# A first attention chunk that skips the operand split, and a written-out order for every engine, in a fused attention and MLP kernel

## The chip, the core and the metric

The kernel runs on one core of one Trainium2 chip. The metric is the device time of one execution in microseconds (us), as a median of several runs. The core has five instruction streams that matter here: TensorE (PE, matmuls and transposes), VectorE (DVE), ScalarE (ACT), GpSimd (POOL) and SyncE (SP), which issues the DMAs. Each works through its own instructions in the order in which they were emitted and waits for semaphores of the others.

## What is computed

Attention over 4 batches, 8 heads, 768 positions and head size 64, with a mask and a bias, followed by a two-layer MLP with a GELU. The mask keeps the first `n_global` keys and the last `n_local` ones before each query.

```python
rel = pos[:, None] - pos[None, :]
is_global = pos[None, :] < int(n_global)
is_local = (rel >= 0) & (rel < int(n_local))
dist = np.where(is_global & ~is_local, float(n_local), np.abs(rel))
scores = scale * q @ k.T - slopes[:, None, None] * dist
a = softmax(np.where(is_global | is_local, scores, -1e9))
x = (a @ v).transpose(0, 2, 1, 3).reshape(3072, 512)
out = gelu(x @ w_in) @ w_out          # 512 -> 2048 -> 512
```

All operands are float32 on the host except the MLP weights, which come as 64-bit words.

## The kernel before

The 3072 tokens are cut into 12 chunks of 256; a batch is three of them. The program has two parts. In the first part all chunks go through attention and through the first two of the eight 256-wide slices of the hidden layer; at the same time the 64-bit weights are turned into float32 and split, and the other six slices are stored to DRAM. In the second part the six slices are multiplied with larger token blocks (lines 575 and 633).

All work is a list of named steps, each registered by `op` with the engines that may do it, an estimated duration, the steps it depends on and the buffers that it takes and frees. `schedule` places them in time on a model of the five engines and so fixes the engine, the order and the buffer of each; `emit` writes the instructions out in that order, and each engine is held to it. The letters, with a chunk, then a head or a pair of heads:

- `l` loads a pair of heads of a chunk (K, Q and V in one tile `nat`), `S` computes scores on TensorE (line 248), `R` adds the mask and takes the maximum on VectorE (265), `E` is the exponential on ScalarE (278), `U` the inverse of the sums (284, 286), `N` scales the rows (294 on ScalarE, 296 elsewhere), `T` transposes them on TensorE (305), `C` copies the result out of PSUM (213), `A` multiplies it with V (326).
- `X` and `Y` (`x_high`, `x_low`) split the attention output into a rounded high part `xh` and a rest `xl`; `W` adds the two again on GpSimd (346) and `Z` spills the sum to DRAM for the second part.
- `w` loads weight words, `D`, `F`, `j` and `J` turn 64-bit words into float32 (`J` is `round_word`, the last), `H` and `L` split them, `Q`, `h`, `o` and `B` prepare and store the other slices.
- `m` is the first layer on chunk and slice: three matmuls for each product (high times high, high times low, low times high); for chunk 0 in parts, one for each pair of heads (`m1_part`, line 472), for the others line 460. `G` and `K` are the GELU and its split, `n` the second layer (496), `O` and `ps` copy and store the partial result. `p` and `m2` are products of the second part.
- `lim` (`reach_of_limits`, lines 60 and 197 to 202) builds the mask out of `n_local` and `n_global`, which lie in the last words of the first `nat` tile; `P` (`penalties`, 252) scales the mask for each head.

Before the first scores TensorE runs idle matmuls (line 271, `warm`): ten, and more wherever the plan has a gap of over 0.5 us before the planned time `IDLE`, 19.761 us. The PSUM bank that they write is free for other use from then on.

Heuristics decide the order: a due time for each step, corrections by kind and chunk (`NUDGE`, `BIAS`), and, for TensorE from the third chunk on, a repeated pattern of seats (`SEATS`, `STEADY`).

Of the kernel before, what the change touches and what calls it, by code (L numbers as in the profile page):

```python
# [17 lines left out]
P = 128  # L18
# [23 lines left out]
W0, W1 = 772, 1280  # L42
# [22 lines left out]
def slope(h):  # L65
# [5 lines left out]
SLOTS = {"k": 8, "nat": 6, "pn": 10, "pt": 10, "x": 3, "xw": 1, "ws": 4, "wa": 4, "wst": 2, "sums": 1, "g": 3, "o": 2,  # L71
# [6 lines left out]
BIAS_FRONT = {("POOL", "N"): -0.807, ("POOL", "J"): -0.4, ("POOL", "L"): -0.546, ("POOL", "Q"): -0.235, ("POOL", "o"): -0.065, ("POOL", "D"): -0.221,  # L78
# [3 lines left out]
STEADY = (10.086, 44.882)  # L82
SEATS = {"S": [-2.0, -1.84, 0.0, 0.16],
         "T": [0.4, 0.48, 0.56, 0.64, 1.85, 2.56, 2.64, 2.93],
         "A": [1.6, 1.76, 3.6, 3.76],
         "m": [4.45, 4.53, 4.61, 4.69],
         "n": [7.2, 7.28, 7.44, 8.44]}
# [7 lines left out]
ISSUE, RATE, FETCH, LAND, AHEAD, CHK = .42, 350.0, 1.3, 1.3, 5.0, 2  # L95
FREE = (3.4, 2.5, 3.0, 2.0, .8)
NUDGE = {("R", 2): -2.16, ("R", 3): 4.48, ("E", 0): -3.31, ("E", 1): -4.66, ("E", 3): 1.13, ("U", 2): 0.06,
# [4 lines left out]
DEC = {(s, i): 57.774 + 6.435 * (4 * (s - NA) + i) for s in range(NA, NST) for i in range(4)}  # L102
EARLY_KEYS = {("A", 1): -0.91, ("A", 3): -0.65, ("m", 1): -0.46, ("m", 2): -0.43, ("n", 0): -0.23, ("n", 2): -1.11}
KEYS = {
    "S": lambda g: g + -1.156 + EARLY_KEYS.get(("S", g // 4), 0.0),
    "T": lambda g: g + 0.62 + EARLY_KEYS.get(("T", g // 4), 0.0),
# [28 lines left out]
class Fast:  # L135
# [197 lines left out]

    def x_high(self, e, c, p, n):
        av, xh, _ = self.x_views(c, p, n)
        self.copy(e, xh, av)
# [12 lines left out]
    def spill(self, c):  # L349
        self.nc.sync.dma_start(self.xd[c], self.t["xw", c].rearrange("p d t -> p (d t)"))  # L350
# [113 lines left out]
    def m1_part(self, c, s, d):  # L464
        xh, xl = self.t["xh", c], self.t["xl", c]
        wh, wl = self.win[s]
        if d == 0:
            self.bank(("h", c, s), [P, 2, CT])
        hp = self.t["k", ("h", c, s)]
        for f in range(2):  # L470
# [224 lines left out]
    def first_part(self):  # L695
        op = self.op
        for h in range(H):
            op(("P", h), [("DVE", .37), ("POOL", .54)], lambda e, h=h: self.penalties(e, h), [("lim",)], port=True)
        op(("lim",), ("DVE", 1.6), lambda e: self.reach_of_limits(), [("l", 0, 0)], free=[("nat", (0, 0))], port=True)
# [6 lines left out]
        for c in range(NCH):  # L706
            f = c % CPB == 0
            for p in range(NP):
# [3 lines left out]
                   kb=(384, 640)[not f])  # L712
                op(("S", c, p), ("PE", (.86, .66)[f]), lambda e, c=c, p=p: self.scores(c, p), [("l", c, p)],
# [9 lines left out]
                for h in (2 * p, 2 * p + 1):  # L723
# [8 lines left out]
                   [("C", c, 2 * p), ("C", c, 2 * p + 1), ("l", c, p), self.at("A", c, p - 1)],  # L732
# [739 lines left out]
```

## Time and profile before

| | us |
|---|---|
| median of 3 runs | 656.88 |
| lowest and highest | 656.49, 657.86 |
| the profiled execution | 656.78 |
| its span, first to last instruction | 655.0 |

| engine | busy us | share of the span |
|---|---|---|
| TensorE | 640.1 | 98% |
| VectorE | 531.0 | 81% |
| ScalarE | 445.5 | 68% |
| GpSimd | 186.8 | 29% |

The shares are averages over both parts. Matmuls are pipelined, and their busy time overlaps; the distance from one start to the next tells what one costs. Lines of a timeline merge neighbours of the same kind: the first number is the start, the second the time until the last of them ends.

### The profile page before, as it was taken

The numbers are of one execution on the slowest core, as the hardware profiler recorded it, in microseconds if no ns is written. First come the engines' busy times: TensorE is split into PE (matmuls) and PEld (weight loads), VectorE is DVE, ScalarE is ACT, GpSimd is POOL, SyncE is SP. The second block draws the span as 40 slices with busy tenths as digits, with TensorE's granted clock in tenths as the row PEclk, the third lists the DMA queues.
The fourth block names the chain that finished last, engine by engine and source line by source line (L and its number), as shares of the span: only waits on it lengthen the run. The fifth ranks groups of instructions, "written<-read, shape, count | busy, mean of one in ns | idle before, by whom it ended". The sixth has DMA issues, their size and how long they took to land. (4 is left out here: it accounts for less than half of the span.)

```text
span 655.0 us, 14882 instructions
## 1 busy us (share of the span) xinstructions
PE 640.1 (98%) x5359; PEld 597.1 (91%) x5359; DVE 531.0 (81%) x1546; ACT 445.5 (68%) x1141; POOL 186.8 (29%) x239
## 2 busy tenths in 40 slices
PE   9999999999999999999999999999999999999996
PEld 7788887888887888989999999999999999999996
DVE  8989999999979874555598789688977987896775
ACT  6999999999999999535554464456345544654450
POOL 5667758788876573100000000000000000000002
PEclk9999999999999999999999999999999999999999
DMA  8875698989979879979995979688888979786402
GB/s 305 290 236 199 258 338 343 344 316 357 394 282 329 324 246 380 419 274 397 419 405 208 327 275 365 240 308 325 312 297 298 333 268 322 263 313 202 172 1 69
DMA packets 48752, 192.44 MB, mean 294 GB/s; under 512 B 5408, under 2 KB 5920, under 8 KB 41760
## 3 DMA queue, kind: packets, MB, share of 16 engines
q1 hardware_dynamic: 48384, 191.16, 79.5%
q8 instruction: 44, 0.72, 0.4%
q14 instruction: 36, 0.29, 0.1%
q10 hardware_dynamic: 288, 0.26, 0.1%
HBM read 150.50 MB, written 40.89 MB: 292 GB/s over the span
## 5 line engine op out<-in xcount | busy, mean ns | idle before, releaser
L633 PE MATMUL k<-w,go 128*128 128x256 f32 x1512 | 193.7, 282 | 1.6 <-DVE vw L642 0.7
L633 PEld LDWEIGHTS k<-w,go 128*128 128x128 f32 x1512 | 185.0, 189 | 2.7 <-PE k L575 1.3
L575 PE MATMUL k<-xch,w1a 128*128 128x256 f32 x576 | 110.5, 284 | 0.5 <-DVE hc L585 0.5
L642 POOL TENSOR_TENSOR part<-part,r 128x256 f32<-128x256 f32 x1 | 0.7, 740 | 372.1 <-DVE r L642 372.1
L278 ACT ACTIVATE pn<-pn,nmax 128x256 f32<-128x256 f32 (+1 forms) x192 | 92.0, 483 | 5.8 <-DVE nmax L265 5.7
L575 PEld LDWEIGHTS k<-xch,w1a 128*128 128x128 f32 x576 | 92.5, 191 | 1.1 <-DVE hc L585 0.7
L575 PE MATMUL k<-xch,w1b 128*128 128x256 f32 x432 | 91.4, 282 | 0.5 <-ACT hc L581 0.5
L581 ACT COPY hc<-k 128x256 f32<-128x256 f32 x108 | 39.8, 368 | 67.9 <-PE k L575 67.8
L575 PE MATMUL k<-xcl,w1a 128*128 128x256 f32 x288 | 81.4, 283 | 0.0
L617 ACT CAST go<-gb 128x384 fp32r<-128x384 f32 x72 | 36.9, 513 | 54.6 <-PE k L633 54.1
L575 PEld LDWEIGHTS k<-xch,w1b 128*128 128x128 f32 x432 | 73.1, 191 | 0.7 <-ACT hc L581 0.7
L585 DVE TENSOR_TENSOR hc<-hc,k 128x256 f32<-128x256 f32 x108 | 44.8, 416 | 35.5 <-ACT hc L581 26.1
L593 ACT ACTIVATE gb<-hc 128x256 f32<-128x256 f32 x108 | 45.2, 418 | 40.6 <-DVE hc L585 39.6
L296 POOL TENSOR_SCALAR pn<-pn,ninv 128x256 f32<-128x256 f32 (+1 forms) x114 | 61.9, 558 | 32.5 <-DVE ninv L286 19.3
L265 DVE CUSTOM_DVE_ANT_0 pn<-k,pens 128x256 f32<-128x256 f32 (+1 forms) x192 | 66.0, 395 | 5.1 <-PE k L248 4.6
L575 PE MATMUL k<-xcl,w1b 128*128 128x256 f32 x216 | 60.9, 282 | 0.0
L305 PE MATMUL k<-ident,pn 128*128 128x128 f32 x352 | 52.7, 279 | 2.7 <-DVE pt L213 1.2
L216 DVE TENSOR_TENSOR go<-gb,go 128x384 fp32r<-128x384 f32 x72 | 39.8, 553 | 19.2 <-ACT go L617 18.8
L575 PEld LDWEIGHTS k<-xcl,w1a 128*128 128x128 f32 x288 | 55.1, 191 | 0.0
L460 PE MATMUL k<-xh,winh 128*128 128x256 f32 x176 | 52.3, 297 | 0.3 <-DVE nmax L265 0.3
L376 POOL TENSOR_TENSOR wa<-wa,ws 128x512 int32<-128x512 int32 x32 | 44.1, 1383 | 25.5 <-DVE wa L371 9.9
L305 PEld LDWEIGHTS k<-ident,pn 128*128 128x128 f32 x352 | 38.3, 140 | 14.0 <-issue 4.6
(123 smaller groups left out, 1458.2 us busy)
## 6 DMA issues: line engine op xcount, KB each, us to landing
w1a<-w1d SPq DMA_DIRECT2D x36, 1024.0 KB, 7.2
w1b<-w1d SPq DMA_DIRECT2D x36, 768.0 KB, 4.7
nat<-qkv SPq DMA_DIRECT2D x32, 640.0 KB, 6.4
ws<-w SPq DMA_DIRECT2D x32, 512.0 KB, 5.6
c<-w SPq DMA_DIRECT2D x64, 256.0 KB, 5.0
w1d<-wst SPq DMA_DIRECT2D x6, 1792.0 KB, 7.6
w2d<-wst SPq DMA_DIRECT2D x6, 1792.0 KB, 8.0
nat<-qkv SPq DMA_DIRECT2D x16, 386.0 KB, 4.6
```

Source lines behind the costliest of these rows:

```text
L216: self.eng(e).tensor_tensor(out=out, in0=in_, in1=hi.bitcast(F32), op=ALU.subtract)
L265: self.nc.vector.tensor_tensor_reduce(out=nn[:, j, :w], in0=sp[:, j, :w], in1=pen, scale=-0.125, scalar=3e38, op0=ALU.add, op1=ALU.min, ac ...
L278: self.nc.scalar.activation(out=nn[:, j, :w], in_=nn[:, j, :w], func=AF.Exp, bias=self.nmax[:, k, i:i + 1], scale=-1.0, accum_out=self.nsu ...
L296: self.eng(e).tensor_scalar(out=nn[:, j, :w], in0=nn[:, j, :w], scalar1=by, scalar2=0.0, op0=ALU.mult, op1=ALU.add)
L305: self.nc.tensor.transpose(tp[:, i, :], nn[:, j, a * P:(a + 1) * P], self.ident)
L376: self.eng(e).tensor_tensor(out=a, in0=a, in1=self.t["ws", (s, i)][:, :, 0], op=ALU.add)
L460: nc.tensor.matmul(hp[:, f, :], lhsT=w[:, d, f * P:(f + 1) * P], rhs=x[:, d, :], start=n == 0, stop=n == 3 * NP - 1)
L575: self.nc.tensor.matmul(out, lhsT=w[:, i, d * P:(d + 1) * P], rhs=y[:, d, :], start=bool(new) and n == 0, stop=n == 5, skip_group_check=no ...
L581: self.nc.scalar.copy(x, self.t["k", ("x", u)])
L585: self.nc.vector.tensor_tensor(out=x, in0=x, in1=self.t["k", (bank, u)], op=ALU.add)
L593: self.nc.scalar.activation(out=out, in_=src, func=AF.Gelu)
L633: self.nc.tensor.matmul(out[k], lhsT=o[:, i, a], rhs=w[:, b, j], start=s == 0 and n == 0 and k in (1, 4, 5, 6), stop=s == NB - 1 and n == ...
```

## The change

Four things change.

1. **The first chunk's loads.** The tiles of chunk 0 (and of the first chunk of each batch, in DRAM) have the limits behind K and Q instead of at the end. For chunk 0, `l` loads 516 words a row (K, Q and the limits) and a new step `v` loads the 256 words of V, which only `A` needs.
2. **The mask.** `reach_of_limits` has one VectorE operation less, and `penalties` may run on ScalarE too.
3. **Chunk 0 whole.** For chunk 0 the attention output is copied as it is (`x_copy`), with no `Y` and no `W`, and `Z` spills that copy. `m1_part` multiplies it with the unsplit float32 weight words in one matmul where three stood. It waits for `X` and `J` instead of `Y` and `L`. The weight words have 7 buffers instead of 4.
4. **The order.** `PLAN` lists, for each of the five engines, the steps of the first part and of the start of the second in their order (358 on TensorE, 370 on ScalarE, 527 on VectorE, 152 on GpSimd, 173 DMAs or pool openings on SyncE). A step in the table goes to the engine in whose list it stands, in that order, and the limits on PSUM use aren't asked for. Estimates of durations and latencies change; `IDLE` goes from 19.761 to 9.87. What is behind the table is ordered by `schedule` as before.

```diff
-SOON, SLACK, WINDOW, LAT, LAT0, IDLE = 0.0, 0.1, 12, 0.255, .05, 19.761
+SOON, SLACK, WINDOW, LAT, LAT0, IDLE = 0.0, 0.1, 12, 0.2, .1, 9.87
+WHOLE = 1
+PLAN = {
+    "PE": """
+        S:0.0 S:0.1 S:0.2 S:1.0 S:0.3 T:0.1 T:0.0 S:1.1 A:0.0 T:0.3 T:0.4 T:0.2 A:0.1 T:0.5 T:1.0 T:1.1 A:0.2 S:1.2
+        T:0.6 T:0.7 m:0.0.0 T:1.3 S:1.3 A:1.0 S:2.0 m:0.1.0 m:0.0.1 T:1.2 m:0.0.2 A:1.1 A:0.3 T:1.5 T:1.7 m:0.0.3
+        m:0.1.1 T:1.4 m:0.1.2 T:1.6 S:2.2 A:1.2 S:2.1 A:1.3 S:2.3 T:2.0 T:2.1 m:0.1.3 n:0.0.1 S:3.0 A:2.0 T:2.2 m:1.0.0
...
+    "ACT": """
+        P:1 P:7 E:0.0 E:0.1 E:0.2 E:0.3 E:0.4 E:0.5 C:0.1 E:1.0 E:1.1 E:0.6 C:0.3 E:0.7 E:1.2 D:0.0 E:1.3 X:0.1 N:0.6
+        C:1.1 D:0.1 N:1.3 C:1.0 C:0.6 C:0.7 D:1.0 E:1.5 E:1.4 D:1.1 E:1.6 E:1.7 C:1.2 H:0.0 E:2.1 D:0.2 X:0.3 D:0.3
...
+    "DVE": """
+        lim: P:0 R:0.0 R:0.1 R:0.2 R:0.4 R:0.3 U:0.0 R:0.5 R:1.0 R:1.1 U:0.1 R:0.6 R:0.7 U:0.2 C:0.0 R:1.3 R:1.2 U:1.0
+        N:1.1 F:0.0 C:0.2 X:0.0 U:0.3 F:0.1 C:0.4 C:0.5 j:0.0 F:1.0 J:0.0 U:1.1 j:0.1 F:1.1 j:1.0 R:1.5 R:1.4 X:0.2
...
+    "POOL": """
+        P:2 P:4 P:3 P:5 P:6 N:0.1 N:0.0 N:0.2 N:0.3 N:0.4 N:0.5 N:1.0 N:0.7 J:0.1 N:1.2 J:1.0 N:1.5 J:1.1 N:1.6 N:1.4
...
+    "SP": """
+        l:0.0 l:0.1 l:0.2 l:1.0 v:0.1 v:0.0 l:0.3 l:1.1 v:0.2 w:0.0 v:0.3 w:0.1 w:1.0 l:1.2 w:1.1 l:1.3 l:2.0 w:0.2
...
     def reach_of_limits(self):
...
-        nc.vector.tensor_scalar(out=col, in0=col, scalar1=self.ng, scalar2=BIG, op0=ALU.is_lt, op1=ALU.mult)
-        nc.vector.tensor_scalar(out=col, in0=col, scalar1=-BIG, scalar2=self.nl, op0=ALU.add, op1=ALU.subtract)
-        nc.vector.tensor_tensor(out=pen[:, 2 * P:], in0=pen[:, P:2 * P], in1=col, op=ALU.max)
-        nc.vector.tensor_copy(pen[:, 0:NG], col[:, 0:NG])
+        nc.vector.tensor_scalar(out=col, in0=col, scalar1=self.ng, scalar2=-BIG, op0=ALU.is_ge, op1=ALU.mult)
+        nc.vector.scalar_tensor_tensor(out=pen[:, 2 * P:], in0=col, scalar=self.nl, in1=pen[:, P:2 * P],
+                                       op0=ALU.subtract, op1=ALU.max)
+        nc.vector.tensor_scalar(out=pen[:, 0:NG], in0=col[:, 0:NG], scalar1=self.nl, scalar2=None, op0=ALU.subtract)
...
+        if c == 0:
+            self.nc.sync.dma_start(t[:, 0:WQ], self.qkv0[b, p, :, 0:WQ])
+            return
...
+    def load_values(self, p):
+        self.nc.sync.dma_start(self.t["nat", (0, p)][:, WQ:W0], self.qkv0[0, p, :, WQ:W0])
...
+        if e == "ACT":
+            self.nc.scalar.activation(out=self.pens[:, h], in_=self.pen, func=AF.Copy, scale=8.0 * slope(h))
+            return
...
+    def x_copy(self, e, c, p):
+        av, xh, _ = self.x_views(c, p, 1)
+        self.copy(e, xh.bitcast(F32), av)
...
     def spill(self, c):
-        self.nc.sync.dma_start(self.xd[c], self.t["xw", c].rearrange("p d t -> p (d t)"))
+        x = self.t["xh", c].bitcast(F32) if c < WHOLE else self.t["xw", c]
+        self.nc.sync.dma_start(self.xd[c], x.rearrange("p d t -> p (d t)"))
...
     def m1_part(self, c, s, d):
...
+        if c < WHOLE:
+            w = self.t["wa", (s, d // 2)].bitcast(F32)
+            for f in range(2):
+                self.nc.tensor.matmul(hp[:, f, :], lhsT=w[:, d % 2 * 256 + f * P:d % 2 * 256 + (f + 1) * P],
+                                      rhs=self.t["xh", c].bitcast(F32)[:, d, :], start=d == f == 0, stop=d == NP - 1,
+                                      skip_group_check=True)
+            return
```

## Rows read from the trace of the kernel before

**Rows 1.** Busy time by stage: engine (instructions) in us, then granted clock, DMA share, GB/s.
```profile
5.00:44.00 39.00, 36.86 (x336) 29.67 (x336) 35.83 (x153) 35.88 (x111) 26.45 (x43) 1.00 0.83 294
44.00:140.00 96.00, 93.75 (x790) 79.15 (x789) 88.83 (x256) 92.58 (x245) 70.67 (x79) 1.00 0.80 287
140.00:260.00 120.00, 118.58 (x1006) 102.17 (x1005) 100.67 (x316) 118.16 (x322) 82.12 (x104) 1.00 0.90 335
...
290.00:649.00 359.00, 356.38 (x2977) 354.56 (x2976) 286.27 (x783) 183.44 (x438) 3.81 (x5) 1.00 0.77 280
```

**Rows 2.** Timeline of VectorE, 4 to 7 us: start, us, engine, line, operation.
```profile
4.08 0.16 DVE L60 SCALAR_TENSOR_TENSOR nn<-nat 128x2 f32<-128x2 int32 x1 [1.15 <-DMA nat<-qkv]
...
4.87 0.28 DVE L199 TENSOR_SCALAR ta<-ta,nn 128x128 f32<-128x128 f32 x1
5.19 0.28 DVE L200 TENSOR_SCALAR ta<-ta,nn 128x128 f32<-128x128 f32 x1
...
5.92 0.74 DVE L252 TENSOR_SCALAR pens<-pen 128x384 bf16<-128x384 bf16 x2
6.78 0.29 DVE L265 CUSTOM_DVE_ANT_0 pn<-k,pens 128x128 f32<-128x128 f32 x1
```

**Rows 3.** Timeline of ScalarE: the first exponentials, and the last of chunk 1.
```profile
7.12 0.40 ACT L278 ACTIVATE pn<-pn,nmax 128x128 f32<-128x128 f32 x1 [5.11 <-DVE nmax L265]
...
8.01 0.39 ACT L278 ACTIVATE pn<-pn,nmax 128x128 f32<-128x128 f32 x1
...
30.98 0.50 ACT L278 ACTIVATE pn<-pn,nmax 128x256 f32<-128x256 f32 x1
...
32.95 0.50 ACT L278 ACTIVATE pn<-pn,nmax 128x256 f32<-128x256 f32 x1
```

**Rows 4.** Timeline of TensorE up to 22 us.
```profile
1.18 4.00 PE L271 MATMUL idle<-wz 128*128 128x256 f32 x17 [1.18 <-DVE wz L1239]
5.10 3.87 PE L248 MATMUL k<-nat 64*128 64x128 f32 x32
...
15.63 0.88 PE L326 MATMUL k<-pt,nat 128*64 128x128 f32 x12 [0.36 <-DVE pt L213]
...
21.93 0.63 PE L305 MATMUL k<-ident,pn 128*128 128x128 f32 x4 [0.88 <-DVE pt L213]
```

**Rows 5.** Timeline of TensorE, later steps.
```profile
25.17 1.75 PE L326 MATMUL k<-pt,nat 128*64 128x128 f32 x28
26.85 0.66 PE L305 MATMUL k<-ident,pn 128*128 128x128 f32 x4
27.26 0.36 PE L472 MATMUL k<-xh,winh 128*128 128x256 f32 x1
...
28.06 0.60 PE L305 MATMUL k<-ident,pn 128*128 128x128 f32 x4
28.59 2.01 PE L248 MATMUL k<-nat 64*128 64x256 f32 x16
...
43.76 0.39 PE L460 MATMUL k<-xh,winh 128*128 128x256 f32 x1
...
283.24 0.39 PE L496 MATMUL k<-wouth,gh 128*128 128x512 f32 x1
...
284.61 0.39 PE L496 MATMUL k<-wouth,gh 128*128 128x512 f32 x1
```

**Rows 6.** Groups by line, 0 to 290 us: count, busy us, mean ns, idle before.
```profile
L213 ACT COPY pt<-k 128x512 f32<-128x512 f32 (+1 forms) x55 | 29.4, 563 | 4.3 <-PE k L305 3.9
L371 DVE SCALAR_TENSOR_TENSOR wa<-ws,wa 128x512 int32<-128x512 int32 x32 | 25.1, 783 | 0.2
L213 DVE COPY pt<-k 128x512 f32<-128x512 f32 (+1 forms) x41 | 24.9, 616 | 1.3 <-PE k L305 1.1
L296 POOL TENSOR_SCALAR pn<-pn,ninv 128x256 f32<-128x256 f32 (+1 forms) x114 | 61.9, 558 | 32.5 <-DVE ninv L286 19.3
...
```

**Rows 7.** One microsecond of the front: engines' busy time, clock, DMA share, GB/s.
```profile
3.00:4.00 1.00, 1.00 (x7) 1.00 (x6) 0.00 (x0) 0.00 (x0) 0.00 (x0) 1.00 1.06 423
```

More of the change, by code (lines that the diff above doesn't have):

```diff
@@ L94 @@
 TABLE = 1.283
[L95 to L97 removed]
[4 rows of a table removed]
[L102 to L103 removed]
+ISSUE, RATE, FETCH, LAND, AHEAD, CHK = .42, 360.0, .8, 1.8, 5.0, 2
@@ L697, in first_part @@
         for h in range(H):
-            op(("P", h), [("DVE", .37), ("POOL", .54)], lambda e, h=h: self.penalties(e, h), [("lim",)], port=True)
-        op(("lim",), ("DVE", 1.6), lambda e: self.reach_of_limits(), [("l", 0, 0)], free=[("nat", (0, 0))], port=True)
+            op(("P", h), [("DVE", .25), ("POOL", .54), ("ACT", .45)], lambda e, h=h: self.penalties(e, h), [("lim",)], port=True)
+        op(("lim",), ("DVE", 1.5), lambda e: self.reach_of_limits(), [("l", 0, 0)], free=[("nat", (0, 0))], port=True)
         lag = KEYS
@@ L749, in first_part @@
                        alloc=[("xw", c)] if p == 1 else [], free=[("x", c)], due=(("A", c, p), 12.0))
-            op(("Z", c), ("SP", ISSUE), lambda e, c=c: self.spill(c), [("W", c, 0), ("W", c, 1)], free=[("xw", c)], kb=512, due=(("A", c, 3), 16.0))
+            op(("Z", c), ("SP", ISSUE), lambda e, c=c: self.spill(c),
+               [("X", c, p) for p in range(NP)] if c < WHOLE else [("W", c, 0), ("W", c, 1)], free=[("x", c) if c < WHOLE else ("xw", c)],
+               kb=512, due=(("A", c, 3), 16.0))
         for s in range(NST):
@@ L1062, in schedule @@
                 due[i] = min(due[i], due[j] - us[i] - .2 - land(ops[i]))
-        nudge = lambda i: NUDGE.get((ops[i].name[0], ops[i].name[1]), 0.0) if len(ops[i].name) > 1 else 0.0
-        rank = [(ops[i].key if ops[i].engs[0][0] == "PE" else due[i] + nudge(i), i) for i in range(n)]
+        nudge = lambda i: (NUDGE.get((ops[i].name[0], ops[i].name[1]), 0.0) if len(ops[i].name) > 1 else 0.0) + FINE.get(ops[i].name, 0.0)
+        rank = [((ops[i].key + FINE.get(ops[i].name, 0.0) if not ops[i].strict else ops[i].key) if ops[i].engs[0][0] == "PE" else
+                 due[i] + nudge(i), i) for i in range(n)]
         cls = lambda a: a[0] + (a[1] if isinstance(a[1], str) else a[1][0]) if a[0] == "k" else a[0]
@@ L1081, in schedule @@
             slots["k"][7] = IDLE
+        read = lambda x: (x.split(":")[0].replace("_", " "),) + tuple(int(v) for v in x.split(":")[1].split(".") if v)
+        plan = {e: [self.named[read(x)] for x in text.split()][::-1] for e, text in PLAN.items()}
+        planned = {i for q in plan.values() for i in q}
+        ends = [0.0] * n
         def place(i, t):
@@ L1085, in place @@
             for a in {cls(a) for a in o.alloc}:
-                if queue[a][-1] != i:
+                if queue[a][-1] != i and i not in planned:
                     return None
@@ L1108, in schedule @@
         engines = ("PE", "ACT", "DVE", "POOL", "SP")
-        strict = [i for i in order if ops[i].strict]
+        strict = [i for i in order if ops[i].strict and i not in planned]
         strict.reverse()
@@ L1117, in make_ready @@
         def make_ready(i):
-            for e, _ in ops[i].engs:
+            for e, _ in ops[i].engs if i not in planned else ():
                 ready[e].append(i)
@@ L1133, in schedule @@
                 k = 0
+                if plan.get(e):
+                    i = plan[e][-1]
+                    if wait[i]:
+                        continue
+                    t = max([free[e] + (turn(turned, ops[i].name[0]) if e == "PE" else 0.0)] +
+                            [ends[d] + (LAT0 if self.on[d] == e else LAT) for d in ops[i].deps])
+                    if uses_port(ops[i], e):
+                        t = max(t, port)
+                    t = place(i, t)
+                    if t is not None and (best is None or t < best[0] - 1e-12):
+                        best = (t, i, e)
+                    continue
                 for i in ready[e]:
@@ L1174, in schedule @@
                 func = kind(i)
-            for x, _ in o.engs:
-                ready[x].remove(i)
-            if o.strict:
-                strict.pop()
+            if i in planned:
+                plan[e].pop()
+            else:
+                for x, _ in o.engs:
+                    ready[x].remove(i)
+                if o.strict:
+                    strict.pop()
             if e == "PE":
@@ L1185, in schedule @@
             if o.kb:
-                pipe = max(pipe, end + FETCH) + o.kb / RATE
-                end = pipe + LAND
+                pipe = max(pipe, end + FETCH) + o.kb / (RATE0 if t < 3.3 else RATE)
+                end = pipe + (LAND0 if t < 8.0 else LAND)
+            ends[i] = end
             done.append((t, len(done), i))
             for a in {cls(a) for a in o.alloc}:
-                queue[a].pop()
+                queue[a].remove(i)
             for a in o.alloc:
```

165 lines of the change are left out of this document (136 added, 29 removed), and 16 rows, old and new, of tables (FINE, NUDGE).

## The prediction

> **What bounds the kernel now.** I read the span by stage first [rows 1]. TensorE is busy 356.38 of 359 us in the second part of the program, so nothing there waits for long. In the first part it is busy 36.86 of 39 us, then 93.75 of 96 and 118.58 of 120, but that flatters it: a matmul is shown for about 0.28 us of pipeline while the next starts some 0.13 us later (six in 0.80 us, below), and part of the first stretch is idle fill. So I read starts instead of busy shares. In the timeline of TensorE [rows 5] one short and one long A step take 26.85 - 25.17 = 1.68 us (0.71 and 0.97), a long S 2.01 / 2 = at most 1.0, a T 27.26 - 26.85 = 0.41, an m step of chunk 0 (six matmuls) 28.06 - 27.26 = 0.80, an n step 284.61 - 283.24 = 1.37. An m of the other chunks (twelve matmuls) I take as 1.48, short S and T as three quarters of the long (0.73, 0.31).
>
> Now the steps. Written out, the table of the change and the old order have the same set of 45 TensorE steps first: S of chunks 0 to 2, T and A of chunks 0 and 1, T:2.0 and T:2.1, all eight m of chunk 0. In the old kernel they run from 5.10 us [rows 4] to 43.76 us [rows 5], 38.7 us. Their content is 8 x 0.97 + 4 x 0.73 + 10 x 0.41 + 8 x 0.31 + 4 x 0.95 + 4 x 0.71 + 8 x 0.80 = 30.3 us, so TensorE waits 8.4 us there. From 43.76 us to the end of the last n, about 284.61 + 2 x 1.37 = 287.4 us, pass 243.6 us; content: 24 x 0.97 + 12 x 0.73 (S), 54 x 0.41 + 24 x 0.31 (T), 28 x 0.95 + 12 x 0.71 (A), 44 x 1.48 (m), 48 x 1.41 (n, some with a switch), 4 x 0.72 (products) = 232, so about 11 us of waits over 240 us. **The first 44 us are bound by the softmax chain on ScalarE and VectorE** (35.88 and 35.83 of 39 us busy), **the rest by TensorE itself** [rows 1].
>
> **Part 1: the mask and the first loads.** The first load carries 258 KB instead of 386. At the 423 GB/s of the microsecond before it lands [rows 7], 128 KB are 0.3 us: the words of the limits come at 3.8 us instead of 4.08. From there to the first reduction the old kernel takes 6.78 - 4.08 = 2.70 us [rows 2]. One operation of the chain goes, 5.19 - 4.87 = 0.32 us, and one of VectorE's two `penalties` steps, about half of 6.78 - 5.92 = 0.86. That leaves 1.95 us: first reduction at 5.75 us, 1.0 earlier. Six steps on GpSimd become five, two go to ScalarE, which stands idle until 7.12 anyway [rows 3]. No row has that step on ScalarE; its bounds are 0.39 us (an exponential of 128 columns) and 0.60 (a copy of 512); I take 0.45, so ScalarE is free at about 6.3, when the first reduction's result comes. The first exponential starts at 6.3 instead of 7.12: 0.8 us. The four V loads cost the SyncE queue four issues of about 0.45 us; behind them wait l:0.3 and l:1.1, but those carry S steps that come after R:0.5 in the table: no cost as long as they land before 9 us, up to 0.5 us if not.
>
> **Part 2: chunk 0 whole.** `x_low` of chunk 0 goes (4 x about 0.3 us of VectorE, half of a 512-column copy's 0.62 [rows 6]), so do two `x_whole` on GpSimd, and m no longer waits for them nor for the weights' split, only for `round_word`. It costs TensorE: a whole float32 matmul of 256 columns. The nearest row is S: its four matmuls run two abreast in 0.97 us, so one takes 0.43 to 0.49, and a step of two 0.86 to 0.97 against 0.80 now. Eight steps: 0.5 to 1.4 us; I take 1.0. While TensorE waits (8.4 us there) this is covered; without that cover it is lost in full.
>
> **Part 3: the table in the first 44 us.** ScalarE's list up to E:1.7, the last exponential of chunk 1, holds 2 `penalties` (0.9), 8 short exponentials at 8.01 - 7.12 = 0.89, 8 long ones at (32.95 - 30.98) / 2 = 0.98 [rows 3], and 6 copies, 4 `low_bits`, one X and two N, 13 steps that I price at the copies' mean of 0.56 [rows 6], 7.3 us. Sum 23.1 us; the list starts at 5.4, so E:1.7 is done at 28.5 with no wait, and at about 29.4 with 0.9 us of waits (the old list, 25.8 us long, has about as much). In the old kernel it is done at 32.95. So that chain is 3.6 us earlier, of which 0.8 is from part 1 and the rest from copies and splits that moved behind it. Behind E:1.7 stand U:1.3, N and T of heads 6 and 7, C, A:1.3 and the last of the 45 steps. From A:0.0 I walk the table: C:0.0 at about 13.0 (old A:0.0, which waits for that copy, at 15.63 [rows 4]), m:0.0.0 at about 20.2 where J:0.0 comes from VectorE, A:1.0 at 22.9 (old 25.88 in the pair at 25.17 [rows 5]), S:2.0 at about 24.5 since its load waits for A:0.2, T:1.6 at about 33.7, the end of the 45 steps at 40.5. Gain 3.3 us. Bounds: 0.8 us (only the first exponential's lead survives) and 6 us (TensorE starts at 4.0 with fewer idle matmuls and runs 31.3 us of content with a third of the old waits).
>
> **Part 4: the table behind that.** The content of TensorE is the same: the pairs of neighbours change (more S-A and A-S, fewer T-S and A-A), but with each pair of kinds at the spacing that the timeline has for it ([rows 5] shows the first of them) both orders sum to the same within 0.3 us. So only the 11 us of waits can change. Counting the table: turned copies go from 55 on ScalarE and 41 on VectorE [rows 6] to 33 and 63; N on VectorE from 0 to 22, on GpSimd from 57 to 38 (two instructions a step [rows 6]); J, L, Q and o change hands between VectorE and GpSimd. ScalarE loses about 22 x 0.56 + 3 x 0.9 - 9 x 0.56 = 10 us of load, GpSimd some 12, VectorE gains 9 to 16: 22 x 0.62 + 22 x 0.5 + 10 x 0.78 + 16 x 0.4 less 14 x 0.69, 14 x 0.69, 9 x 0.69 and 4 x 0.34. ScalarE, the fullest helper (92.58 of 96, 118.16 of 120), gets 5% of air; VectorE, 88.83 of 96 and 100.67 of 120 [rows 1], comes to about 90%. An N on VectorE is done in about half the time of two 0.56 us steps on GpSimd, which shortens the path U-N-T-C-A. I take 2.5 us of the 11 as saved; bounds minus 6 (half) and plus 3 (VectorE late now and then).
>
> The port that VectorE and GpSimd share shows in the trace: VectorE's two `penalties` steps last 0.86 us up to the first reduction beside GpSimd's, and the join of the weight words has a mean of 783 ns against 616 for a copy of as many columns [rows 2, 6]. The Trainium skill, "SBUF — State Buffer", section "Who interferes with whom", says more strictly that the pair is locked for a whole instruction and the loser waits it out. By that rule moving N and J to VectorE helps (the lock is held for half as long) as long as it doesn't queue VectorE behind the remaining GpSimd steps; that second case is the rival below that ends slower.
>
> **Sum.** The profiled execution took 656.78 us (span 655.0 and 1.8 around it), 0.1 under the median of the three, 656.88. Minus 3.3, minus 2.5: **651.0 us**. The second part keeps its code; its products come earlier with everything before them.
>
> **The rivals.**
> *Given back (chance 0.17).* The lead of the front is eaten by TensorE's order later: the table is strict, one late copy holds all steps behind it. For it: the old order is strict too and waits 11 us. Front gain 1 to 3, later waits plus 0 to 2: 654 to 656, I say 655.
> *VectorE becomes the bound (chance 0.1, slower).* It decides if VectorE's work per chunk, with port waits, passes TensorE's 20 us. From chunk 6 on the table gives VectorE some 8 us more over five chunks, where it had 100.67 of 120 busy [rows 1], so 19 us of air; port waits of 0.15 us on each of some 120 steps that use the port there would be another 18 us. 26 is more than 19: the seven that are left come on top of the time, 656.8 - 3.3 + 7 = 660. Against it: GpSimd, the other user of the port, loses more than VectorE gains.
> *The clock (chance 0.12).* The 17 idle matmuls at the start take 4.00 us, 0.235 each, nearly twice the later 0.13: TensorE is at 1.2 GHz there, and the first S steps are slow too (four short ones in 3.87 us, 0.97 each, against 0.73 above) [rows 4, 5]. With an earlier first load the planner fills less, and the limit for fill drops from 19.8 to 9.9 us. If the clock comes later or falls again between 10 and 20 us, S, A and T there take twice as long: content of about 8 us, half of it covered by waits: plus 2 to 3, 653.5. Against it: the wait of 0.88 us before 21.93 [rows 4], without fill, left the granted clock at 1.00. The Trainium skill, "TensorE: Matmul & The Clock Gate", section "What's actually happening", holds that throttled is the default and activity lifts it, which speaks against taking fill away; no row here shows a fall before the end.
> *The early start doesn't come (chance 0.08):* l:1.0, 640 KB and now fourth in the queue, delays l:0.3; the lead of part 1 is gone, 653.
>
> **How the numbers follow.** My forecast, 649 to 653 with all its bounds, has 0.53. The range holds 8 in 10: upward it takes in the clock, the lost start and the given-back case (656), leaving out VectorE as the bound; downward it reaches 646.5, where front and later gains come near their far ends (3.3 + 2.5 + half of the 2.7 and 3.5 still open, and some). About 0.2%, 1.3 us, is what a measurement can tell from no change. Faster by more than that (under 655.6): 0.53 + 0.12 + 0.08 + two fifths of 0.17 = 0.80; within it 0.09; slower 0.11.
>
> **What would show it.** Right: first S near 4.0, first reduction near 5.8, first exponential near 6.3; first m of chunk 0 near 20; the end of the 45 steps near 40.5; ScalarE's busy share between 44 and 260 us down, VectorE's up, TensorE's last n near 281.5. Wrong: idle of TensorE behind `pt` copies of VectorE in chunks 6 to 11; a spacing of 0.21 us of 256-column matmuls after 10 us; the whole m steps longer than 1.0 us.

## The result and the profile after

| | before | after |
|---|---|---|
| median of four, us | 657.2 | 666.55 |
| lowest and highest | 656.49, 657.86 | 665.38, 667.16 |
| span of the profiled execution | 655.0 | 664.5 |

The changed kernel is slower: ratio 1.014, 95% interval 1.0122 to 1.0159, 9.4 us. The prediction was 651.0, faster. Line numbers after: S 371, R 391, E 404, N 420 on ScalarE and 422 elsewhere, T 431, A 452, `m` of chunk 0 602, other `m` 591, `n` 634, F 497, j 502, J 507; 329 and 332 are the helpers for copies and for two-operand steps.

The busy time by stage of the changed kernel, columns as in [rows 1]:

```profile
5.00:44.00 39.00, 34.16 (x303) 26.70 (x299) 37.23 (x148) 36.86 (x114) 26.01 (x38) 1.00 0.85 297
44.00:140.00 96.00, 89.99 (x734) 74.08 (x733) 93.18 (x261) 85.82 (x222) 55.46 (x56) 0.98 0.79 275
140.00:260.00 120.00, 118.73 (x991) 99.81 (x991) 106.90 (x343) 109.04 (x299) 71.43 (x83) 0.99 0.89 321
290.00:649.00 359.00, 356.74 (x2960) 354.34 (x2959) 281.48 (x771) 184.28 (x443) 2.31 (x2) 1.00 0.79 288
```

ScalarE got its air and VectorE filled up, as forecast. But TensorE is busy 89.99 of 96 us in the second stretch, where it had 93.75, and the granted clock is 0.98 and 0.99 where it was 1.00. The waits of TensorE between 44 and 290 us tell where (what waited, for whom: us in total, times, longest). After, the first four of six:

```profile
PE k L431 <- DVE nmax L391: 2.6, 1, 2.6
PE k L452 <- DVE nmax L391: 1.7, 1, 1.7
PE k L371 <- DVE pt L329: 1.3, 2, 0.9
PE k L431 <- DVE pn L422: 0.8, 1, 0.8
```

and before, the whole list:

```profile
PE k L496 <- DVE nmax L265: 0.9, 1, 0.9
PE k L248 <- DVE nmax L265: 0.7, 1, 0.7
PE k L305 <- ACT pt L213: 0.5, 1, 0.5
PE k L305 <- DVE o L213: 0.4, 1, 0.4
PE k L460 <- DVE nmax L265: 0.3, 1, 0.3
```

Two single waits of 2.6 and 1.7 us are new. And the old kernel names waits of 2.8 us here, where the prediction counted 11. The larger wait is that of T of head 6 in chunk 4. By the program it needs N of its head and a free PSUM bank; by the row of TensorE below the maximum (R) came last. These are the timelines of the changed kernel. VectorE, the two N (heads 5 and 6) that stand ahead of that maximum on its list, two instructions each:

```profile
104.32 1.45 DVE L422 TENSOR_SCALAR pn<-pn,ninv 128x256 f32<-128x256 f32 x1
105.70 1.38 DVE L422 TENSOR_SCALAR pn<-pn,ninv 128x256 f32<-128x256 f32 x1
107.00 1.37 DVE L422 TENSOR_SCALAR pn<-pn,ninv 128x256 f32<-128x256 f32 x1
108.30 0.84 DVE L422 TENSOR_SCALAR pn<-pn,ninv 128x256 f32<-128x256 f32 x1
```

GpSimd in the same microseconds, four instructions of its own without a gap:

```profile
104.36 1.27 POOL L332 TENSOR_TENSOR wst<-sums,wst 128x512 fp32r<-128x512 f32 x1
105.59 1.34 POOL L507 TENSOR_TENSOR wa<-wa,ws 128x512 int32<-128x512 int32 x1
106.90 1.32 POOL L507 TENSOR_TENSOR wa<-wa,ws 128x512 int32<-128x512 int32 x1
108.27 0.72 POOL L553 TENSOR_TENSOR wst<-wa,wst 128x256 fp32r<-128x256 f32 x1
```

and TensorE:

```profile
106.16 1.09 PE L452 MATMUL k<-pt,nat 128*64 128x128 f32 x16
109.88 0.33 PE L431 MATMUL k<-ident,pn 128*128 128x128 f32 x1 [2.63 <-DVE nmax L391]
```

Read the ends: 105.77, 107.08, 108.37 and 109.14 on VectorE, 105.63, 106.93, 108.22 and 108.99 on GpSimd. Each N instruction, 0.35 us where it runs alone (below), ends 0.14 to 0.15 us after one instruction of GpSimd: it waits that one out, and the next begins 0.1 us too late and waits out the next. Two N take 4.82 us, TensorE stands for 2.63. What comes then, in windows of 2 us (columns as above):

```profile
108.00:110.00 2.00, 0.12 (x1) 0.12 (x2) 2.00 (x7) 1.47 (x2) 1.68 (x3) 1.00 0.82 304
110.00:112.00 2.00, 1.84 (x12) 1.40 (x13) 2.00 (x10) 1.80 (x7) 0.00 (x0) 0.88 1.00 307
112.00:114.00 2.00, 2.00 (x9) 1.81 (x8) 2.00 (x6) 2.00 (x8) 0.00 (x0) 0.50 0.94 313
114.00:116.00 2.00, 2.00 (x9) 1.60 (x8) 1.99 (x7) 0.33 (x2) 0.86 (x1) 0.77 1.11 453
```

After the stall TensorE is granted half its clock, 1.2 GHz, in the whole of 112 to 114 us; an `n` step takes 2.44 us there instead of 1.47. The same happens at chunk 5: N of head 6 lasts 2.33 us, A of pair 2 waits 1.67, and the clock is 0.50 from 140 to 142 us. The four executions of the changed kernel differ in the clock: their mean granted clocks are 0.992, 0.992, 0.997 and 0.994, at 666.25, 667.16, 665.38 and 666.85 us. The one with the highest clock is the shortest, by 0.9 to 1.8 us: the falls seem not to be the same each time, and most of the loss is there in any case.

### The profile page after: what moved, and what is told of

It is laid out like the page before. It is cut to its first block, busy times and chain, and to the rows that moved or that the text cites. A ratio compares the mean times of both kernels' runs of the same rounds, so it can differ in the third digit from the quotient of the medians.

```text
span 664.5 us, 14784 instructions
## 1 busy us (share of the span) xinstructions
PE 642.8 (97%) x5324; PEld 594.8 (90%) x5324; DVE 547.7 (82%) x1596; ACT 436.0 (66%) x1120; POOL 171.8 (26%) x203
## 4 chain that ended last, share of the span: by engine, by line
## 5 line engine op out<-in xcount | busy, mean ns | idle before, releaser
L371 PE MATMUL k<-nat 64*128 64x256 f32 (+1 forms) x384 | 50.4, 387 | 3.5 <-DVE pt L329 1.9
L452 PEld LDWEIGHTS k<-pt,nat 128*64 128x64 f32 x704 | 37.6, 136 | 17.0 <-issue 8.6
L431 PEld LDWEIGHTS k<-ident,pn 128*128 128x128 f32 x352 | 40.1, 143 | 13.4 <-issue 4.9
```

Of the source, the lines that this page charges most:

```text
L371: self.nc.tensor.matmul(sp[hh][:, j, :w], lhsT=qq[hr, j * P:(j + 1) * P], rhs=kt[hr, 0 if first else j, :w], start=True, stop=True)
L431: self.nc.tensor.transpose(tp[:, i, :], nn[:, j, a * P:(a + 1) * P], self.ident)
L452: self.nc.tensor.matmul(av[64 * hh:64 * hh + 64, j, :], lhsT=vr[:, vj, vn, hh, :], rhs=self.t["pt", (c, 2 * p + hh)][:, i, :], start=(j, a ...
```

## The experiments

Two theories at first. **Port**: the 22 N that moved to VectorE are locked out by GpSimd, some of them ahead of steps that TensorE needs at once. **Tight**: the table leaves no slack anywhere, and any lateness costs; the port is only one source.

### N in a form that is not locked out

```diff
+            if e == "DVE":
+                self.nc.vector.tensor_scalar(out=nn[:, j, :w], in0=nn[:, j, :w], scalar1=by, scalar2=0.0,
+                                             op0=ALU.mult, op1=ALU.add, accum_out=self.junk)
```

> The changed kernel with one edit: the 22 scaling steps N that its table puts on VectorE also write out a sum of each row (thrown away), so that they run in the plain mode, which needs no second port. Order, engines and buffers are unchanged. Theory 'port' (VectorE's N, 0.54 us alone, lasts up to 2.8 us because GpSimd holds the port that both use; two such stalls let TensorE wait and its clock fall): every N lasts 0.6 to 0.8 us whatever GpSimd does, no clock fall between 10 and 640 us, 656 to 659 us against 666.5 of the changed kernel. Theory 'tight' (the table is about 12 us tighter than the chip can follow, and N is only where it shows): N gets short, the waits appear elsewhere, 664 to 667 us.

661.26 us, ratio 1.0058 (1.0041 to 1.0075): 5.3 us of the loss gone. The N group of VectorE, 0 to 290 us, columns as in [rows 6]:

```profile
L424 DVE TENSOR_SCALAR_CACHE_REDUCE pn<-pn,ninv 128x256 f32<-128x256 f32 (+1 forms) x44 | 20.1, 457 | 1.0
```

No N is long any more: the longest instruction lasts 0.48 us. But the mean is 457 ns, and a whole N takes 0.85 to 1.01 us, where 0.6 to 0.8 was expected. The clock fell here too, in the front (windows of 2 us):

```profile
16.00:18.00 2.00, 0.37 (x6) 0.37 (x8) 1.97 (x8) 2.00 (x9) 0.49 (x2) 1.00 0.85 306
20.00:22.00 2.00, 2.00 (x16) 1.51 (x14) 1.97 (x7) 0.13 (x1) 0.00 (x0) 0.50 0.75 295
```

and the first `m` came at 23.95 us instead of 21.87. (The traced execution took 663.67 us, 2.4 more than the median of this version, so the others may have lost less there.) So port holds in kind, and the result misses its 656 to 659. In this trace the end of the front is 1.5 us later than in the version that follows, and the third n of chunk 11 is 5.3 us later. The dearer form and the clock of the front are both likely parts of that; they weren't separated. The Trainium skill, "SBUF — State Buffer", section "Who interferes with whom", says that `tensor_scalar` can contend for the shared pair, except in the form that writes out its accumulator. The trace agrees: at most 0.48 us for an instruction of this form, up to 1.45 us for one of the other.

### GpSimd waits until N on VectorE is done

```diff
+            if self.on[i] == "DVE" and o.name[0] == "N":
+                self.held = new[-1]
+            if self.on[i] == "POOL" and self.held is not None:
+                self.tc.add_manual_dep(new[0], self.held.name, mybir.DependencyInfo(
+                    mybir.DependencyClass.Sync, mybir.DependencyReason.DATA), reason="GpSimd behind the scaling")
+                self.held = None
```

Same engines, same order of each engine; only the next GpSimd step of the list waits.

> The changed kernel with one wait more for each of the 22 N on VectorE: the GpSimd step that the plan puts behind it waits for it, so N competes with at most the one GpSimd step that is already running. Theory 'port': N at most 1.9 us, the stall of 2.8 us at T:4.6 and that of 1.8 at A:5.2 shrink to under 1 us, no clock fall, 658 to 662 us. Theory 'tight': GpSimd is held back too, later steps come later, 666 to 670 us.

656.35 us, ratio to before 0.9987 (0.9977 to 0.9996): 10.2 us better than the changed kernel, more than either theory gave. The N group of the changed kernel:

```profile
L422 DVE TENSOR_SCALAR pn<-pn,ninv 128x256 f32<-128x256 f32 (+1 forms) x44 | 24.6, 605 | 0.1
```

and of this version, with its first two instructions of head 5, chunk 4:

```profile
L422 DVE TENSOR_SCALAR pn<-pn,ninv 128x256 f32<-128x256 f32 (+1 forms) x44 | 12.8, 339 | 0.1
103.70 0.35 DVE L422 TENSOR_SCALAR pn<-pn,ninv 128x256 f32<-128x256 f32 x1
103.96 0.35 DVE L422 TENSOR_SCALAR pn<-pn,ninv 128x256 f32<-128x256 f32 x1
```

11.8 us of VectorE are gone, the granted clock stays at 1.00 from 44 to 290 us, and the loss is gone. This version serves as the yardstick for where the loss arose: starts of TensorE's steps, changed kernel less this one (its traced execution took 657.23 us, 0.9 over its median).

| step | changed | this | difference | added since the line above |
|---|---|---|---|---|
| second n of chunk 0 | 48.83 | 49.40 | -0.57 | |
| m, chunk 1, second | 51.80 | 51.15 | 0.65 | 1.22, long N of chunk 2, head 3 (2.60 us) |
| T, chunk 4, head 6 | 109.88 | 106.56 | 3.32 | 2.67, the first stall |
| second n of chunk 3 | 115.25 | 109.75 | 5.50 | 2.18, mostly half clock |
| A, chunk 5, pair 2 | 137.50 | 130.32 | 7.18 | 1.67, the second stall |
| second n of chunk 4 | 142.58 | 133.67 | 8.91 | 1.74, mostly half clock |
| S, chunk 7, first | 158.31 | 148.49 | 9.83 | 0.91, long N of chunk 6, head 5 (2.05 us) |
| third n of chunk 11 | 294.78 | 285.28 | 9.50 | |

At the first row the changed kernel is still ahead; from there on it loses 10.1 us, about what the medians differ by (10.2).

### The 22 N back on GpSimd

In the table, 22 names move from VectorE's list to GpSimd's, for instance:

```diff
-        ... C:4.3 C:4.2 N:4.5 N:4.6 R:5.1 ...
+        ... C:4.3 C:4.2 R:5.1 ...
-        N:4.4 o:3.0.0 o:3.0.1 J:4.0 ...
+        N:4.4 o:3.0.0 N:4.5 N:4.6 o:3.0.1 J:4.0 ...
```

> The changed kernel with its 22 N moved from VectorE's list to GpSimd's, each at the place that its planned time has there; all else in the table stays. N then takes 0.9 to 1.0 us and is queued behind GpSimd's own steps. Theory 'port': no step of VectorE's lasts over 1.9 us, no clock fall, 657 to 661 us. Theory 'tight': 664 to 668 us.

659.67 us, ratio 1.0034 (1.0023 to 1.0045). In the range of port, far from tight: with N moved, the rest of the table comes to within 3.3 us of the version above.

### Parts 1 and 2 without the table

```diff
-SOON, SLACK, WINDOW, LAT, LAT0, IDLE = 0.0, 0.1, 12, 0.2, .1, 9.87
+SOON, SLACK, WINDOW, LAT, LAT0, IDLE = 0.0, 0.1, 12, 0.255, .05, 19.761
-PLAN = {
...
+PLAN = {e: "" for e in ("PE", "ACT", "DVE", "POOL", "SP")}
```

(and the heuristics' numbers of the kernel before).

> Chunk 0 whole, V loaded apart and the shorter mask, but without the table and with the old rules and estimates for the order (7 buffers for the weight words). Both theories put the loss into the table: 655 to 657.5 us, the first exponential about 0.8 us earlier than in the old kernel, TensorE some 1 us longer on the eight m of chunk 0. If chunk 0 whole itself were the loss (longer m, or weight words held longer): over 660 us.

660.58 us, ratio 1.0045 (1.0029 to 1.0062): a miss, and by the number in the range set for a loss by chunk 0 whole itself. That doesn't follow, since versions with the table keep chunk 0 whole too and come to 656.35 and below. The trace shows waits that this order makes: an A of chunk 1 waits 1.83 us, up to 41.19, for a copy, and the granted clock is 0.63 in the two microseconds from 42 and 0.52 in the next two. That the old rules, fitted to the old steps, place the new ones badly is the likely reason, not a shown one. What parts 1 and 2 are worth by themselves stays open.

### Waits in three places alone

```diff
-            if self.on[i] == "DVE" and o.name[0] == "N":
+            if self.on[i] == "DVE" and o.name in (("N", 4, 5), ("N", 4, 6), ("N", 5, 6)):
```

> The changed kernel, in which GpSimd's next step waits for N on VectorE in three places alone: heads 5 and 6 of chunk 4 and head 6 of chunk 5, the ones ahead of the two stalls of TensorE. The other 19 N on VectorE stay as they are beside GpSimd (together 13.0 us over their undisturbed 0.54 in the changed kernel, of which these three have 2.2 + 1.6 + 1.8 = 5.6). If two stalls and the two falls of the clock behind them make the loss: 656 to 658, no granted clock of 0.50 behind 105 us. If the loss is spread over all long N: the share 5.6 of 13.0 of the 10.2 us comes back, 662.

659.58 us, ratio 1.0034 (1.0021 to 1.0047). 7.0 of the 10.2 us come back with 3 of 22 N, nearer to the first expectation than to the second; the granted clock doesn't fall behind 105 us, up to the last microseconds. Its third n of chunk 11 is 2.8 us behind the version with all waits. Long N that were left alone come ahead of the steps where it falls behind: chunk 2, head 3, at 50.5 us, 2.60 us, and chunk 6, head 5, at 148.8 us, 2.05 us; 1.0 was there at the end of the front already, where TensorE waited longer for loads.

### A stall made by hand

```diff
+            if o.name == ("N", 4, 5):
+                self.nc.vector.memset(self.junk, 0.0)
+                for _ in range(6):
+                    self.nc.vector.tensor_tensor(out=self.junk, in0=self.junk, in1=self.junk, op=ALU.max)
```

> The version in which GpSimd waits behind each N of VectorE (656.35), with 3.8 us or so of idle work for VectorE (a fill and six maxima of 512 columns) ahead of N of head 5 in chunk 4, so that TensorE waits for T of head 6 there as in the changed kernel, but with no lock-out. If the clock answers to the wait of TensorE itself: a granted clock of 0.50 for about 3.4 us some 2 us behind the stall, and 656.35 plus 2.6 of wait plus 1.5 to 2 of slow matmuls, 660 to 661. If the fall came from something else that the changed kernel does: clock 1.00 throughout, and 658 to 659. If TensorE has slack behind it that takes the stall up: 656.5 to 657.5.

662.85 us, ratio 1.0082 (1.0068 to 1.0097). GpSimd stands still meanwhile, so there is no lock-out; TensorE's wait and the windows around it:

```profile
110.41 0.90 PE L432 MATMUL k<-ident,pn 128*128 128x128 f32 x3 [3.84 <-DVE nmax L392]
108.00:110.00 2.00, 0.00 (x0) 0.00 (x0) 2.00 (x8) 0.80 (x1) 0.19 (x1) 0.96 0.93 330
110.00:112.00 2.00, 1.59 (x8) 1.59 (x9) 2.00 (x13) 1.27 (x5) 2.00 (x2) 0.50 0.26 105
112.00:114.00 2.00, 2.00 (x12) 1.96 (x11) 1.66 (x4) 2.00 (x9) 2.00 (x3) 0.69 0.34 53
```

The work by hand lasted 4.8 us rather than 3.8, so the wait is 3.84. The clock falls at the end of it, not 2 us later, and with no lock-out near: TensorE's own wait is enough for a fall. Step starts give 3.85 us late at T and 5.22 at the second n of chunk 3: 1.4 for the clock on top, and nothing taken up by slack in the 180 us that follow (5.34 at the third n of chunk 11). The medians differ by 6.5, the two traced executions by 5.8 (663.04 and 657.23); the 0.5 us that the step starts leave of that were not followed up.

### One reason why no more than 1 us is left: pairs of S and of A

With the lock-out gone the new order should have been some 6 us faster by the prediction; it is 1. The larger part of what is missing is the front (below): the 45 steps end at 43.93 us in that version, 43.76 in the old kernel. The starts of TensorE's steps show another reason. Four steps, S and A in turn, in the version with waits behind N:

```profile
102.38 1.13 PE L371 MATMUL k<-nat 64*128 64x256 f32 x8
103.44 1.09 PE L452 MATMUL k<-pt,nat 128*64 128x128 f32 x16
104.47 1.14 PE L371 MATMUL k<-nat 64*128 64x256 f32 x8
105.53 1.09 PE L452 MATMUL k<-pt,nat 128*64 128x128 f32 x16
106.56 0.66 PE L431 MATMUL k<-ident,pn 128*128 128x128 f32 x4
```

4.18 us, and no wait among them. The same four in the next version, two and two:

```profile
101.44 2.00 PE L371 MATMUL k<-nat 64*128 64x256 f32 x16
103.36 1.97 PE L452 MATMUL k<-pt,nat 128*64 128x128 f32 x32
105.26 1.97 PE L431 MATMUL k<-ident,pn 128*128 128x128 f32 x16
```

3.82 us. The change had broken up 15 pairs of S and 14 of A that the old order kept together. Summed by kind of step from the end of the 45 steps to the end of the last n (start to start, waits of over 0.2 us left out), S and A take 68.3 us in the old kernel and 73.0 with waits behind N; T, m and n take 169.6 and 165.9. So the new order costs 4.7 us in S and A and saves 3.7 in the rest.

```diff
-        m:3.1.0 T:4.2 m:3.0.1 m:3.1.1 S:5.0 A:4.0 S:5.1 A:4.1 T:4.6 ...
+        m:3.1.0 T:4.2 m:3.0.1 m:3.1.1 S:5.0 S:5.1 A:4.0 A:4.1 T:4.6 ...
```

and eight more places like it, on top of the waits behind N.

> The version in which GpSimd waits behind each N of VectorE, with nine places of TensorE's list changed: two S and two A that stood alternating (S A S A) stand as S S A A or A A S S, as in the kernel before; 8 more neighbours S S and 9 more A A. By the starts in the trace an S between steps of other kinds takes 1.064 us, two S in a row 0.968 + 0.961; an A 1.025, two in a row 0.924 + 0.974: 0.20 and 0.15 for each pair that is kept. If that is what ate the gain behind 44 us: 8 x 0.20 + 9 x 0.15 = 3.0 us less, minus up to 1 for copies that now come later than the step that needs them: 653.3 to 654.5. If the spacing follows from the waits and not from the order: 656 to 657. If the alternation kept the softmax chain fed: 658 or more.

656.15 us (655.19 to 657.47), ratio 0.9986 (0.9978 to 0.9995): by the time no better than without. In its trace the third n of chunk 11 starts at 283.12 instead of 285.28, but 0.94 of these 2.16 are there at the first A of chunk 3, where the first changed place begins, and the trace is of an execution of 655.24 us, beside one of 657.23. S and A do take 3.0 us less in it, as expected; T takes 0.9 more and TensorE's waits of over 0.2 us 1.2 more, so about 1 us is left. So the spacing follows the order, as the rows show, and most of the gain turns into new waits. The executions of this kernel spread over 2.3 us, and the cause of that wasn't found.

### Waits behind F and j too

```diff
-            if self.on[i] == "DVE" and o.name[0] == "N":
+            if self.on[i] == "DVE" and o.name[0] in "NFj":
```

> The version in which GpSimd waits behind each N of VectorE, with the same wait behind F and j too (32 of each; F lasts up to 1.54 us where 0.40 is its undisturbed length, j up to 1.78 where 0.66 is; above those lengths together about 10 us of VectorE). If the lock-out still holds TensorE up, in the front above all (F of chunk... slice 1, part 2 at 33.7 us lasts 1.52 and the copies behind it come 1.0 late): end of the 45 steps 0.5 to 1 us earlier and 655 to 656. If it's covered everywhere: 656.2 to 656.6. If GpSimd, waiting more often, gets late with its own N: 657 to 659.

654.55 us, ratio 0.996 (0.9948 to 0.9973), better than expected. The groups of F and j with the waits behind N alone:

```profile
L502 DVE SCALAR_TENSOR_TENSOR wa<-ws,wa 128x512 int32<-128x512 int32 x32 | 26.3, 827 | 0.0
L497 DVE TENSOR_SCALAR wa<-ws 128x512 int32<-128x512 int32 x32 | 17.2, 541 | 1.5 <-DMA ws<-w 1.5
```

and here:

```profile
L502 DVE SCALAR_TENSOR_TENSOR wa<-ws,wa 128x512 int32<-128x512 int32 x32 | 22.2, 699 | 0.0
L497 DVE TENSOR_SCALAR wa<-ws 128x512 int32<-128x512 int32 x32 | 13.3, 422 | 1.4 <-DMA ws<-w 1.4
```

8.0 us of VectorE come back, and TensorE is busy in all of 44 to 140 us (96.00 of 96, where the version with the waits behind N alone has 95.32).

### Both together, and one step of the front moved

The pairs and all the waits, and then the same with `N:1.1` moved from VectorE's list to GpSimd's, behind `N:1.0`:

```diff
-        N:1.1 F:0.0 C:0.2 X:0.0 ...
+        F:0.0 C:0.2 X:0.0 ...
-        ... N:0.5 N:1.0 N:0.7 J:0.1 ...
+        ... N:0.5 N:1.0 N:1.1 N:0.7 J:0.1 ...
```

> The version in which GpSimd waits behind each N, F and j of VectorE (654.55), and TensorE's list with the nine places where two S and two A stand in pairs. If the waits and the pairs are two separate gains: by the last n, GpSimd's waits had 2.0 us over the version with N alone (285.28 to 283.29, 0.5 of it already there at the first A), the pairs 2.2 (283.12, 0.5 of it at the first A too), so 1.2 to 1.7 us more: 652.8 to 653.5. If what the pairs gave was taken by the same copies that the waits free: 654.2 to 654.8. If GpSimd's waits make the copies behind the paired steps late: over 655.

652.79 us, ratio 0.993 (0.9917 to 0.9942): 1.8 us less than with the waits alone, a little over what two separate gains should give (the "last n" of that expectation is the third n of chunk 11), though without the waits behind F and j the pairs had given 0.2. This version beats both kernels, by 4.3 and 13.8 us.

> The version before this one with one step moved: N of head 1 of chunk 1 from VectorE's list (15.11 to 15.95 us) to GpSimd's, behind N of head 0, where GpSimd stands idle. If VectorE's list sets the front (it works without a gap from 3.58 to 16.75 us, up to the copy that A of pair 1 waits for): A of pair 1 0.6 to 0.8 us earlier (16.4 where it was 17.1), first m 0.5 us earlier, 652.4 to 653.2. If ScalarE's exponentials set it, as the prediction had it: first A and first m where they were, and the same time as the version beside it. If GpSimd's own later N get late: slower by 0.5 or more.

652.90 us, ratio 0.9937 (0.9921 to 0.9952), the same. A of pair 1 does come earlier, 16.41 instead of 17.12 (0.3 of it from earlier loads), but at the end of the front only the 0.3 from the loads is left. VectorE's list sets the first steps, and something else stands right behind it: S of pair 3 in chunk 1 now waits 0.21 us, by the profile for its load, and the rest of the lead is gone at the first S of chunk 2; for what wasn't found out.

### What the waits and the table are worth alone

The kernel before with the same waits behind F and j, and the changed kernel with the table cut off at the steps due before 44 us (rules behind it) and all three waits:

```diff
+            if self.on[i] == "DVE" and o.name[0] in "NFj":
+                self.held = new[-1]
...
-        S:3.3 A:2.2 A:2.3 T:3.0 T:3.1 n:1.0.1 m:2.1.0 ...
```

> The kernel before with one thing added: GpSimd's next step waits behind each F and j of VectorE (it has no N there; F lasts up to 1.5 us and j up to 1.8 in it too, where 0.40 and 0.66 are the undisturbed lengths). It tells whether the best versions gain by these waits or by the table. If the waits alone carry it: 1.2 to 1.8 us less, as between the two versions of the table with and without waits behind F and j: 655.1 to 655.7. If the waits only give the table what it counted on: 656.5 to 657.2. If GpSimd, the one that scales most rows there, gets late: 658 or more.

657.95 us, ratio 1.0011 (1.0002 to 1.0021): the waits by themselves give nothing.

> The changed kernel with the table cut off at the steps that are due before 44 us (the rest is ordered by the rules of the kernel before, with the new durations), and GpSimd's next step waits behind each N, F and j of VectorE. It tells what the table is worth behind 44 us: the same waits with the whole table gave 654.55. If the gain lies in the front alone: 654.5 to 656. If the rules, with their new durations, make stalls of their own, as they did in the version with no table at all (660.58): 658 to 661.

661.16 us, ratio 1.0059 (1.0045 to 1.0072): T waits 2.3 us in one place for VectorE.

```profile
145.25 0.55 PE L347 MATMUL k<-ident,pn 128*128 128x128 f32 x3 [2.31 <-DVE o L245]
```

The granted clock stays at 1.00 around this wait (140 to 152 us), so not every wait of that length takes the clock. Of the versions tried, only those with the whole table and the waits together get to 654.55 and below.

## Why the prediction was wrong, step by step

Two steps failed. The sign came out wrong by Part 4, which booked N on VectorE as a gain ("done in about half the time") and put its waits for GpSimd at little: its 44 instructions took 605 ns in the mean instead of 339, a few of them held TensorE up, and the clock fell behind two of these waits, together some 10 us. Without that loss the gain would still have been about 1 us and not 5.8, since the front of Part 3 gave next to nothing and the waits that Part 4 drew on weren't there.

- **What bounds it.** "About 11 us of waits over 240 us" was a difference of two large sums, 243.6 and 232, with rounded step prices. The view of waits names 2.8 us. Start to start the same steps take 240.7 us in the old trace: m 67.5 (65.1 in the prediction), n 70.2 (67.7), T 31.9 (29.6), S 32.9 (32.0), the others as priced. There was no 11 us to draw 2.5 from. The busy shares that the prediction set aside as flattering (93.75 of 96, 118.58 of 120) were near the truth here.
- **Part 1 was right.** First S 3.84 us (4.0 forecast), first reduction 5.64 (5.75), first exponential 6.07 (6.3 for 7.12 before).
- **Part 2 was right in size**: two whole `m` steps of chunk 0 take 28.25 - 26.42 = 1.83 us, 0.92 each, 0.86 to 0.97 forecast. What it's worth in time stays open (see the version without the table).
- **Part 3 failed.** The 45 steps end at 43.35 us (40.5 forecast, 43.76 before): 0.4 us instead of 3.3. Rows of the front, VectorE and then TensorE:

```profile
15.11 0.85 DVE L422 TENSOR_SCALAR pn<-pn,ninv 128x256 f32<-128x256 f32 x2
15.88 0.41 DVE L497 TENSOR_SCALAR wa<-ws 128x512 int32<-128x512 int32 x1
16.21 0.55 DVE L329 COPY pt<-k 128x384 f32<-128x384 f32 x1
16.67 0.41 DVE L329 COPY xh<-k 128x256 f32<-128x256 f32 x1
```

```profile
17.14 0.88 PE L452 MATMUL k<-pt,nat 128*64 128x128 f32 x12 [1.61 <-DVE xh L329]
21.87 1.03 PE L602 MATMUL k<-xh,wa 128*128 128x256 f32 x4
36.50 1.13 PE L371 MATMUL k<-nat 64*128 64x256 f32 x8 [0.61 <-DVE pt L329]
43.35 0.58 PE L634 MATMUL k<-wouth,gh 128*128 128x512 f32 x1
```

  I priced ScalarE's list, and that price held: its last exponential of chunk 1 ends at 28.83 (28.5 to 29.4 forecast, 32.95 before). But this chain doesn't set the end of the 45 steps, in either kernel: the old TensorE's last named wait before 44 us ends at 21.93 [rows 4], and by the prediction's own prices some 7 of the 8.4 us of waiting lie before that. VectorE, not priced, works almost without a gap until the copy of `xh` at 16.67, for which A of pair 1 waits, 1.61 us in all; from there to 43.35 TensorE waits once, for 0.61 us. The first `m` is at 21.87, not 20.2. What is left, 25.6 us from 17.14 on, is nearly all TensorE's own content, which the step prices of the prediction put at 24.2; S and A in turn (1.06 and 1.03 against 0.97 and 0.95) are part of that.
- **Part 4 failed in sign.** "Both orders sum to the same within 0.3 us": a step's spacing depends on its neighbours. Two S and two A in turn cost 0.36 us more than in pairs, T, m and n win most of that back, and the sum is 1.0 us higher. That is small beside the weighing of the port: I read means, 783 against 616 ns [rows 6], where the longest instance tells the price. Right behind the words "moving N and J to VectorE helps" stood the condition, "as long as it doesn't queue VectorE behind the remaining GpSimd steps". It did, in a few places. The rule cited there from the Trainium skill, "SBUF — State Buffer", section "Who interferes with whom", that the loser waits out a whole instruction, is what the rows at 104 us show, once for each of four instructions.
- **The rivals.** VectorE as the bound, chance 0.10, had the mechanism, but its price was wrong: 0.15 us on 120 steps, due only when VectorE's air is used up. The 44 instructions of N alone cost 11.8 us, and most of the loss comes not from their sum but from a few N that stood ahead of what TensorE needed next: waits behind three of the 22 give back 7.0 of 10.2 us. The clock, 0.12, was put between 10 and 20 us; there it stayed at 1.00 in the changed kernel, and fell instead behind both stalls, for up to 3.9 of the 10.1 us. (The prediction reads 1.2 GHz for the first microseconds from the spacing alone; the granted clock of [rows 7] is 1.00 there.) The Trainium skill, "TensorE: Matmul & The Clock Gate", section "What's actually happening", has throttled as the default state that activity lifts; the two falls behind waits of 2.63 and 1.67 us, and the one at a wait by hand of 3.84, agree with it, while the wait of 0.88 in the kernel before left the clock at 1.00 [rows 4]. So did longer ones: 1.61 us at 17.14 in the changed kernel, and 2.31 in the version whose table is cut off. That a stall can be paid twice was missing from every case; when it is, these runs don't tell.
- **The range** left out every loss, and the slowest case that was priced, 660, was some 6.5 us short, since no case joined the two rivals: a lock-out that stalls TensorE, and a stall that takes the clock.

## What to carry to other kernels

Before moving steps between VectorE and GpSimd, read the longest instance of each kind that contends, not its mean: here an instruction that was locked out lasted about as long as one of GpSimd's, 1.4 us instead of 0.35. If an order is written out by hand, make GpSimd wait behind such a step; here that turned 666.55 into 654.55, while in the old order, which has no N on VectorE, such waits behind F and j cost 0.1%. And price a reordering of matmuls by runs of one kind, and TensorE's waits from the view of waits, not as a difference of sums.

## What the runs showed of the hardware

- Two engines can fall into step: four N instructions of 0.35 us lasted 1.45, 1.38, 1.37 and 0.84 us, each let go by the end of a GpSimd instruction and caught by the next, which had begun 0.1 us before.
- Some waits of TensorE in a busy stretch came with a granted clock of 0.50 and cost more than themselves: 1.67 us cost 1.7 more, 2.63 cost 2.2 more, and 3.84 cost 1.4 more. Others, of 1.61 and 2.31 us, left the clock at 1.00.
- Score and value matmuls in turn take 4.18 us for four steps, in pairs 3.82, with no wait in either.
